# Value product and next scores between the halves of h, products of the high part first, one sum on VectorE

## The chip, the cores and the metric

The kernel runs on one core of a Trainium2 chip. The metric is the device time of one execution in microseconds (us), and runs of the kernel before are shown with their median. The engines are named as the trace names them: PE (TensorE's matmuls; PEld is its loading of weights), DVE (VectorE), ACT (ScalarE), POOL (GpSimd) and SP (SyncE, which here only issues transfers). All of them run in order, each its own list of instructions, and wait for one another by semaphores.

## The reference, cut to what matters

```
attention in chunks of 64:  scores = q k^T / 8; attn = softmax(scores); out = attn v
x  = out as (4608 tokens, 512)
h  = x @ w_in                                  # 512 -> 1024
sm = softmax(h);  u = h * sm
ln = (u - mean(u)) / sqrt(var(u) + 1e-6) * g
y  = ln @ w_out                                # 1024 -> 512
z  = y @ w_in2;  z = max(0.01 z, z);  out = z @ w_out2      # 512 -> 2048 -> 512
```

## The kernel before

The work has two parts. The first (attention, h, softmax, norm, y) goes over 36 tiles of 128 tokens, one tile at a time. The second (the last two products) goes over 6 groups of 768 tokens by a scheme of seven products in place of eight; the change doesn't touch it. Every float32 operand of a product is held as two rounded parts, high and low, and each product is made of three: high by high, high by low, low by high.

In the first part a round t of the loop holds work of several tiles at once, in an order that is written out by hand and that each engine keeps:

- `qk_mm(t+2)` (L349) makes scores, `softmax_a` and `softmax_b` (L362 to L373) the probabilities `es`: DVE takes maxima, differences and sums, ACT the exponentials, and POOL the last multiplication (L373, 128x512).
- `pt_mm` (L383) and `pt_copy` (L389, ACT) transpose the probabilities, `pv_mm` (L399) multiplies them by the values, `x_hi` (L413, ACT) and `x_lo` (L417, DVE) split the result x into its high and low part, `xs`. `attend(t)` is `pv_mm(t+1)` and the split, from t = 5 on also the scores, loads and `softmax_a` of tile t+3.
- `ff1_mm(t, half)` (L434) makes h: for t of 2 and more a half is 512 of the 1024 columns; for tiles 0 and 1 it is two of the four blocks of rows of w_in, for both column halves.
- `solu_max`, `solu_a`, `solu_b` (L449, L453, L457, L465) take the maximum of h's row, the exponentials (ACT) and their product with h (`us`, DVE), with sums over each column half in columns 8 to 11 of the small tile `z`. `solu_c` adds these sums of the halves on POOL (L479, two of them: the sum of the exponentials in column 1, that of the products in column 2) and gives the second to ACT, whose square (`sq`, L488) takes it as its bias. `solu_d` finishes the norm on POOL (L494 to L498).
- `lnT_mm` (L509) transposes the normed tile, `lnT_hi` (L520, ACT) and `lnT_lo` (L524, DVE) split it, `y1_group` (L536) makes 128 rows of y for 512 tokens, from t = 5 on one group a round, and ACT copies it out (`ys`, L544).
- In between, weights that arrive as float64 words are converted: ACT `magnitudes` (L101), DVE L108 to L118, POOL `by_g` (L171), ACT and POOL the split of w_out (L124, L125), DVE, ACT and POOL the blocks of the second part's weights (L189 to L195). Some rounds convert two pieces (`DOUBLE`).

Two sets of PSUM banks matter below: the outputs of `lnT_mm` and `y1_group` take turns in two banks called `ef`, and the transposed probabilities and x share one bank called `ptx`. Rounds 5, 9, 13, ... are called late: they copy and split the norm of tile t-2 before the rest, and make the first group of y of a block. The lines that are shown here and those of the profile are the same.

Of the kernel before, what the change touches and what calls it, by code (L numbers as in the profile page):

```python
# [14 lines left out]
ALU = mybir.AluOpType  # L15
# [8 lines left out]
T = NT // P  # L24
# [18 lines left out]
AHEAD = 5  # L43
# [9 lines left out]
def kernel(  # L53
# [252 lines left out]
    with tc.manual_schedule():  # L306

        with ExitStack() as phase:
# [107 lines left out]
                ps, x = x_ps.pop(t), xs[t]  # L416
                dve.tensor_tensor(x[:, 1], ps, x[:, 0].bitcast(F32), op=ALU.subtract)  # L417

            def ff1_mm(t, half):
                if t < 2:  # L420
                    ks, ns = ((0, 1), (2, 3))[half], (0, 1)
                else:
                    ks, ns = range(KD), (half,)
                for n in ns if t >= 2 or half == 0 else ():
                    if t == 1 and n == 1:
                        hs[t, n] = bank("ef", "h_ps")
                    else:
                        hs[t, n] = psh.tile([P, 512], F32, tag="h", name="h_ps")
                x = xs[t]
                for kk in ks:  # L430
                    w = slots["wi1", kk // 2].rearrange("p e (a n f) -> p e a n f", a=2, n=2)
                    for a, b in ((0, 0), (0, 1), (1, 0)):
                        for n in ns:
                            pe.matmul(  # L434
                                hs[t, n],
                                lhsT=x[:, a, kk, :],
                                rhs=w[:, b, kk % 2, n, :],
                                start=(kk == 0 and a == 0 and b == 0),
                                stop=(kk == KD - 1 and a == 1),
                            )  # L440
                if half == 1:
                    del xs[t]

            sol = {}
# [16 lines left out]
            def solu_b(t):  # L461
                z, u = sol[t], us[t]
                for n in range(2):
                    c = slice(n * 512, (n + 1) * 512)
                    dve.scalar_tensor_tensor(  # L465
                        u[:, c],
                        hs.pop((t, n)),
                        1.0 / FF1,
                        u[:, c],
                        op0=ALU.mult,  # L470
                        op1=ALU.mult,
                        accum_out=z[:, 10 + n : 11 + n],
                    )

            def solu_c(t):
                z, u = sol[t], us[t]
                for n in (1, 2):
                    a = 6 + 2 * n
                    pool.tensor_tensor(  # L479
                        z[:, n : n + 1], z[:, a : a + 1], z[:, a + 1 : a + 2], op=ALU.add  # L480
                    )
                pool.tensor_scalar(
                    z[:, 4:5], z[:, 1:2], 1e-9, (1e-6 * FF1 * LN_SCALE) ** 0.5, op0=ALU.add, op1=ALU.mult
                )
                pool.tensor_tensor(z[:, 5:6], z[:, 4:5], z[:, 4:5], op=ALU.mult)
                pool.tensor_scalar_mul(z[:, 0:1], z[:, 2:3], -1.0 / FF1)
                sq = wk.tile([P, FF1], BF16, tag="sq", bufs=1, name="sq")
                act.activation(  # L488
                    sq, u, AF.Square, scale=-float(FF1), bias=z[:, 2:3], accum_out=z[:, 3:4]
                )  # L490
# [63 lines left out]
            def attend(t):  # L554

                pv_mm(t + 1)
                if AHEAD <= t < T - 3:
                    qk_mm(t + 3)
                    load_qk(t + 4)
                x_split(t + 1)  # L560
                if AHEAD <= t < T - 3:
                    softmax_a(t + 3)
# [160 lines left out]
            for t in range(1, T + 2):  # L723
                if t == T:
                    att.close()
                    yp = ctx.enter_context(
                        tc.tile_pool(name="yp", bufs=1, side="right", reuse_waits="tile")
                    )
                    ws = ctx.enter_context(
                        tc.tile_pool(name="ws", bufs=WS, side="right", reuse_waits="tile")  # L730
                    )
                    for n in range(4):
                        y_load(0, n)
                    for _ in range(WS):
                        w_load()
                if t <= AHEAD:
                    load_qk(t + 3)
                load_v(t + 2)
                store_next()
                load_next(owed)  # L740
                owed = 0
                b, g = divmod(t - 5, 4)
                groups = [(b, g)] if 5 <= t < T else []
                if t == T - 1:
                    groups = []
                elif t == T:
                    groups = [(NB - 2, 2), (NB - 2, 3)]
                elif t == T + 1:
                    groups = [(NB - 1, m) for m in range(KD)]
                late = g == 0 or t == T - 1  # L750
                pieces = 0 if t in (1, 4) or t >= T - 2 else 2 if t in DOUBLE else 1
                if 0 < t <= AHEAD:
                    qk_mm(t + 2)
                if 1 <= t <= T:
                    if t < 3:
                        solu_max(t - 1, 0)
                    solu_max(t - 1, 1)
                    solu_a(t - 1)
                if t <= AHEAD:
                    softmax_a(t + 2)  # L760
                if t > AHEAD and not late:
                    take_magnitudes(pieces)
                if 1 < t < T:
                    ff1_mm(t, 0)
                if 1 <= t <= T:
                    solu_b(t - 1)
                if t + 1 < T:
                    pt_mm(t + 1)
                if t + 2 < T:
                    softmax_b(t + 2)  # L770
                if t <= AHEAD or (late and t < T - 1):
                    pt_copy(t + 1)
                if late and t >= 2:
                    lnT_mm(t - 2)
                    lnT_split(t - 2, 0)
                    lnT_split(t - 2, 1)
                if t > AHEAD:
                    if late:
                        take_magnitudes(pieces)
                    convert_a(pieces)  # L780
                    convert_b(pieces)
                if AHEAD < t < T - 1 and not late:
                    pt_copy(t + 1)
                if 1 < t < T:
                    solu_max(t, 0)
                if 1 <= t <= T:
                    solu_c(t - 1)
                    solu_d(t - 1)
                if t == T + 1:
                    y_split(0, 0)  # L790
                    for name in ("s1", "s3", "s2"):
                        y_sum(0, name)
                    y_split(0, 1)
                    y_sum(0, "s4")
                    for k in range(2, 7):
                        y_split(0, k)
                if groups and not late:
                    for bm in groups:
                        y1_group(*bm)
                    if t + 1 < T:  # L800
                        attend(t)
                    if t >= 2:
                        lnT_mm(t - 2)
                        lnT_split(t - 2, 0)
                        lnT_split(t - 2, 1)
                    if t < T:
                        ff1_mm(t, 1)
                    finish(pieces)
                else:
                    if t >= 2 and not late:  # L810
                        lnT_mm(t - 2)
                        for hf in range(2):
                            (lnT_hi if t < AHEAD else lnT_split)(t - 2, hf)
                    if AHEAD < t < T - 1:
                        attend(t)
                    if t < T:
                        ff1_mm(t, 1)
                    if t <= AHEAD:
                        attend(t)
                        if 2 <= t < AHEAD:  # L820
                            for hf in range(2):
                                lnT_lo(t - 2, hf)
                        finish()
                        take_magnitudes(pieces)
                        convert_a(pieces)
                        convert_b(pieces, load=t == AHEAD)
                        owed = pieces if t < AHEAD else 0
                    if t >= AHEAD:
                        finish(pieces)
                    for bm in groups:  # L830
                        y1_group(*bm)
# [295 lines left out]
```

## Time and profile before

| what | value |
|---|---|
| median of 3 runs | 1279.92 us (1279.71 to 1281.45) |
| the profiled execution's own time | 1279.53 us |
| span in its trace | 1277.7 us |
| PE busy | 1234.1 us, 97% of the span |
| DVE, ACT, POOL busy | 891.3, 572.9, 287.5 us |
| end of the first part on PE (first product of the second) | 568.6 us |

The span is the time from the first to the last instruction in the trace; the execution's own time is 1.8 us more. Busy time is summed over instructions of an engine. The second part runs on PE almost without a gap, so what can be seen of waiting lies in the first 569 us. A row of the timeline has the start, the length, the engine, the line and the operation, the tile it writes and those it reads; in brackets stands how long its engine sat idle before it and what ended that.

### The profile page before, as it was taken

How to read it: one execution, taken by the hardware profiler on the slowest of the kernel's cores; microseconds unless marked ns; L12 is line 12 of the kernel's file. 1: busy time of each engine (PE TensorE's matmuls, PEld its weight loads, DVE VectorE, ACT ScalarE, POOL GpSimd, SP SyncE). 2: the span in 40 equal slices, each digit the busy share in tenths (PEclk: the TensorE clock that was granted, in tenths of full speed). 3: DMA queues.
4: the chain of work that ended last, by engine and by line, in shares of the span. 5: the costliest groups of instructions: out<-in, count | busy, mean ns of one | idle time of the engine just before them, and what ended most of it. 6: DMA issues, size and time to landing. Idle time of an engine off the chain costs nothing.

```text
span 1277.7 us, 22962 instructions
## 1 busy us (share of the span) xinstructions
PE 1234.1 (97%) x8554; PEld 1094.5 (86%) x8554; DVE 891.3 (70%) x1567; ACT 572.9 (45%) x1078; POOL 287.5 (22%) x426
## 2 busy tenths in 40 slices
PE   5888999999999999999999999999999999999998
PEld 4666788878878887889989998998899899989987
DVE  8666678887887788445676677567757775775675
ACT  6553545554555555433434344235234433442351
POOL 0244455765664576400000000000000000000000
PEclk8998999999999999999999999999999999999999
DMA  7423355755676564529899988987898899789676
GB/s 246 149 69 116 116 179 169 259 175 172 203 240 199 157 189 151 206 80 325 267 307 295 303 243 257 316 287 241 277 316 257 264 294 304 241 260 300 205 214 198
DMA packets 171070, 288.83 MB, mean 226 GB/s; under 512 B 50000, under 2 KB 80720, under 8 KB 169936
## 3 DMA queue, kind: packets, MB, share of 16 engines
q1 hardware_dynamic: 170592, 286.78, 70.3%
q8 instruction: 69, 1.13, 0.3%
q10 hardware_dynamic: 368, 0.59, 0.1%
q14 instruction: 41, 0.34, 0.1%
HBM read 239.08 MB, written 48.23 MB: 225 GB/s over the span
## 4 chain that ended last, share of the span: by engine, by line
PE 80%; DVE 10%; ACT 4%; DMA 2%; issue 2%; POOL 2%; SPq 0%; POOLq 0%; ACTq 0%
PE h_ps L870 27%; PE o_ps L927 18%; PE y_ps L536 11%; PE o_ps L938 9%; PE h_ps L434 9%; PE x_ps L399 2%; DVE us L465 1%; PE ln_ps L509 1%; DMA kb<-in_k 1%; DVE lnT L524 1%; DVE wf L114 1%; DVE wf L108 1%; POOL es L373 1%; DVE wc L191 1%; DVE st L362 1%
## 5 line engine op out<-in xcount | busy, mean ns | idle before, releaser
L870 PE MATMUL h_ps<-yo,w_s 128*128 128x384 f32 x2016 | 351.0, 334 | 0.0
L870 PEld LDWEIGHTS h_ps<-yo,w_s 128*128 128x128 f32 x2016 | 349.3, 188 | 0.7
L927 PE MATMUL o_ps<-wo_s,yo 128*128 128x512 f32 (+1 forms) x1016 | 262.8, 393 | 0.0
L434 PE MATMUL h_ps<-wi,xs 128*128 128x512 f32 x864 | 214.8, 401 | 12.3 <-ACT xs L413 5.5
L536 PE MATMUL y_ps<-lnT,wo 128*128 128x512 f32 (+1 forms) x888 | 204.7, 387 | 1.1 <-POOL wo L125 0.8
L434 PEld LDWEIGHTS h_ps<-wi,xs 128*128 128x128 f32 x864 | 161.7, 192 | 49.3 <-DVE us L465 6.3
L927 PEld LDWEIGHTS o_ps<-wo_s,yo 128*128 128x128 f32 x1016 | 179.0, 188 | 28.7
L536 PEld LDWEIGHTS y_ps<-lnT,wo 128*128 128x128 f32 x888 | 161.6, 188 | 33.6 <-POOL wo L125 1.3
L938 PEld LDWEIGHTS o_ps<-wo_s,yo 128*128 128x128 f32 x1008 | 144.6, 188 | 15.6
L271 DVE TENSOR_TENSOR yo<-c,yo 128x768 fp32r<-128x768 f32 x144 | 132.5, 952 | 32.0 <-ACT yo L270 32.0
L938 PE MATMUL o_ps<-wo_s,yo 128*128 128x256 f32 x1008 | 149.7, 283 | 0.0
L849 ACT ACTIVATE c<-h_c 128x384 f32<-128x384 f32 x144 | 72.9, 526 | 127.7 <-DVE h_c L881 127.7
L881 DVE TENSOR_TENSOR h_u<-h_ps,h_p 128x384 f32<-128x384 f32 x96 | 53.3, 555 | 105.9 <-PE h_ps L870 99.2
L270 ACT ACTIVATE yo<-c 128x768 fp32r<-128x768 f32 x144 | 113.1, 838 | 7.1 <-DVE c L911 5.5
L488 ACT ACTIVATE sq<-us,z 128x1024 bf16<-128x1024 f32 x36 | 41.4, 1150 | 80.5 <-POOL z L479 80.5
L465 DVE SCALAR_TENSOR_TENSOR us<-h_ps,us 128x512 f32<-128x512 f32 x72 | 48.6, 690 | 35.0 <-ACT us L457 35.0
L373 POOL TENSOR_TENSOR es<-es,st 128x512 f32<-128x512 f32 x33 | 34.6, 1048 | 157.3 <-DVE st L372 148.0
L524 DVE TENSOR_TENSOR lnT<-ln_ps,lnT 128x512 fp32r<-128x512 f32 x72 | 45.8, 680 | 33.9 <-ACT lnT L520 33.9
L457 ACT ACTIVATE us<-h_ps,z 128x512 f32<-128x512 f32 x72 | 48.7, 682 | 39.1 <-DVE z L453 39.1
L270 ACT ACTIVATE yo<-a 128x768 fp32r<-128x768 f32 x36 | 30.0, 841 | 72.6 <-DVE a L265 72.6
L881 DVE TENSOR_TENSOR h_c<-h_ps,h_u 128x384 f32<-128x384 f32 x96 | 53.2, 554 | 13.1 <-PE h_ps L870 11.9
L417 DVE TENSOR_TENSOR xs<-x_ps,xs 128x512 fp32r<-128x512 f32 x36 | 24.7, 687 | 51.4 <-ACT xs L413 51.4
(89 smaller groups left out, 1415.9 us busy)
## 6 DMA issues: line engine op xcount, KB each, us to landing
w_s<-wi_d SPq DMA_DIRECT2D x336, 256.0 KB, 4.0
wo_s<-wo_d SPq DMA_DIRECT2D x168, 512.0 KB, 4.6
wi_d<-wi SPq DMA_DIRECT2D x8, 1792.0 KB, 6.4
wo_d<-wi SPq DMA_DIRECT2D x8, 1792.0 KB, 7.0
raw<-in_w_out SPq DMA_DIRECT2D x24, 512.0 KB, 5.1
raw<-in_w_in SPq DMA_DIRECT2D x23, 512.0 KB, 5.6
vbd<-in_v SPq DMA_DIRECT2D x72, 128.0 KB, 4.6
a<-y_d SPq DMA_DIRECT2D x24, 384.0 KB, 5.3
```

The lines of the kernel that those rows point to most:

```text
L270: act.activation(o[:, 0], x, AF.Copy)
L271: dve.tensor_tensor(o[:, 1], x, o[:, 0].bitcast(F32), op=ALU.subtract)
L434: pe.matmul(hs[t, n], lhsT=x[:, a, kk, :], rhs=w[:, b, kk % 2, n, :], start=(kk == 0 and a == 0 and b == 0), stop=(kk == KD - 1 and a == 1),)
L457: act.activation(u[:, c], hs[t, n], AF.Exp, bias=z[:, 0:1], accum_out=z[:, 8 + n : 9 + n])
L465: dve.scalar_tensor_tensor(u[:, c], hs.pop((t, n)), 1.0 / FF1, u[:, c], op0=ALU.mult, op1=ALU.mult, accum_out=z[:, 10 + n : 11 + n],)
L524: dve.tensor_tensor(dst[:, 1], ps, dst[:, 0].bitcast(F32), op=ALU.subtract)
L536: pe.matmul(ps[:, part], lhsT=w[:, a, kk % 4, m * P : (m + 1) * P], rhs=lnT[:, c, kk, pairs, :][:, part], start=(kk == 0 and a == 0 and c ...
L849: act.activation(blocks[block, j // 2][:, j % 2], src, AF.Prelu, alpha=0.01)
L870: pe.matmul(ps, lhsT=w[:, a, kk * P : (kk + 1) * P], rhs=y[:, c, kk, :], start=(first and kk == 0 and a == 0 and c == 0), stop=(kk == 1 an ...
L881: dve.tensor_tensor(o, ps, x, op=ALU.add)
L927: pe.matmul(ps[:, : 2 * P * (a.stop - a.start)], lhsT=x[:, 0, kk, m * P : (m + 1) * P], rhs=w[:, kk, a].rearrange("p a n -> p (a n)"), sta ...
L938: pe.matmul(sums[p % 2][m][:, : 2 * P], lhsT=x[:, 1, kk, m * P : (m + 1) * P], rhs=w[:, kk, 0], start=False, stop=(i == PAIRS - 1 and kk = ...
```

## The change

Three things are changed. `ff1_mm` runs through its blocks of rows twice, first for the two products of x's high part, then for that of its low part, where it took the three products of a block together. In rounds 2 to 5 `attend(t)` stands ahead of `ff1_mm(t, 1)` where it stood behind it, and in round 1 between the two blocks of that half; the later rounds had it ahead already. The sum of the halves' products (column 2 of `z`) is made on DVE, at the end of `solu_b`, where it was one of POOL's two additions in `solu_c`.

```diff
-            def ff1_mm(t, half):
+            def ff1_mm(t, half, ks=None):
                 if t < 2:
-                    ks, ns = ((0, 1), (2, 3))[half], (0, 1)
+                    ks, ns = ks or ((0, 1), (2, 3))[half], (0, 1)
...
-                for kk in ks:
-                    w = slots["wi1", kk // 2].rearrange("p e (a n f) -> p e a n f", a=2, n=2)
-                    for a, b in ((0, 0), (0, 1), (1, 0)):
-                        for n in ns:
-                            pe.matmul(
...
+                for terms in (((0, 0), (0, 1)), ((1, 0),)):
+                    for kk in ks:
+                        w = slots["wi1", kk // 2].rearrange("p e (a n f) -> p e a n f", a=2, n=2)
+                        for a, b in terms:
+                            for n in ns:
+                                pe.matmul(
...
+                dve.tensor_tensor(z[:, 2:3], z[:, 10:11], z[:, 11:12], op=ALU.add)
 
             def solu_c(t):
                 z, u = sol[t], us[t]
-                for n in (1, 2):
-                    a = 6 + 2 * n
-                    pool.tensor_tensor(
-                        z[:, n : n + 1], z[:, a : a + 1], z[:, a + 1 : a + 2], op=ALU.add
-                    )
+                pool.tensor_tensor(z[:, 1:2], z[:, 8:9], z[:, 9:10], op=ALU.add)
...
-                    if AHEAD < t < T - 1:
+                    if t == 1:
+                        ff1_mm(t, 1, (2,))
                         attend(t)
-                    if t < T:
+                        ff1_mm(t, 1, (3,))
+                    elif t < T - 1:
+                        attend(t)
+                    if 1 < t < T:
                         ff1_mm(t, 1)
                     if t <= AHEAD:
-                        attend(t)
```

On PE, in round 1 and the first half of round 2, before (s_ps are scores, pt_ps the transposed probabilities, h_ps the products of h, x_ps the value product, ln_ps the transposed norm):

```order
L383 MATMUL pt_ps<-ident,es 128x128 x4
L434 MATMUL h_ps<-wi_355,xs 128x512 x12
L399 MATMUL x_ps<-pt,vbd_104 64x64 x16
L349 MATMUL s_ps<-kb_102,qt 64x64 x16
L434 MATMUL h_ps<-wi_173,xs 128x512 x6
L434 MATMUL h_ps<-wi_355,xs 128x512 x6
L383 MATMUL pt_ps<-ident,es 128x128 x4
L509 MATMUL ln_ps<-ident,us 128x128 x8
L434 MATMUL h_ps<-wi_173,xs 128x512 x6
L434 MATMUL h_ps<-wi_355,xs 128x512 x6
L399 MATMUL x_ps<-pt,vbd_105 64x64 x16
L349 MATMUL s_ps<-kb_103,qt 64x64 x16
```

The same place of PE in the changed kernel:

```order
L383 MATMUL pt_ps<-ident,es 128x128 x4
L435 MATMUL h_ps<-wi_355,xs 128x512 x6
L399 MATMUL x_ps<-pt,vbd_104 64x64 x16
L435 MATMUL h_ps<-wi_355,xs 128x512 x6
L349 MATMUL s_ps<-kb_102,qt 64x64 x16
L435 MATMUL h_ps<-wi_173,xs 128x512 x4
L435 MATMUL h_ps<-wi_355,xs 128x512 x4
L435 MATMUL h_ps<-wi_173,xs 128x512 x2
L435 MATMUL h_ps<-wi_355,xs 128x512 x2
L383 MATMUL pt_ps<-ident,es 128x128 x4
L507 MATMUL ln_ps<-ident,us 128x128 x8
L399 MATMUL x_ps<-pt,vbd_105 64x64 x16
```

The value product of the next tile (x_ps) now stands between the halves of h in round 1, and in round 2 right behind the transposed norm, with the second half of h behind it; within a half the eight products of the high part stand ahead of the four of the low part.

On DVE in round 3, from the minimum of the negated maxima to the factors of the probabilities, before:

```order
L453 TENSOR_TENSOR z<-z 128x1
L362 TENSOR_REDUCE st_739<-s_ps 128x4 x2
L365 TENSOR_TENSOR es<-s_ps,st_739 128x4x64 x2
L465 SCALAR_TENSOR_TENSOR us,z<-h_ps,us 128x512 x2
L370 TENSOR_REDUCE st_739<-es 128x8
L371 TENSOR_SCALAR st_739<-st_739 128x8
L372 RECIPROCAL st_739<-st_739 128x8
```

The same place of DVE in the changed kernel:

```order
L454 TENSOR_TENSOR z<-z 128x1
L362 TENSOR_REDUCE st_739<-s_ps 128x4 x2
L365 TENSOR_TENSOR es<-s_ps,st_739 128x4x64 x2
L466 SCALAR_TENSOR_TENSOR us,z<-h_ps,us 128x512 x2
L475 TENSOR_TENSOR z<-z 128x1
L370 TENSOR_REDUCE st_739<-es 128x8
L371 TENSOR_SCALAR st_739<-st_739 128x8
L372 RECIPROCAL st_739<-st_739 128x8
```

One addition of 128x1 (L475) has come in behind the products `us`, ahead of the sum of the probabilities (L370); DVE has 36 of them, one for each tile, and POOL 36 fewer.

On POOL in the same round, the multiplication of the probabilities and what of the norm is queued behind it, before:

```order
L373 TENSOR_TENSOR es<-es,st_739 128x512
L479 TENSOR_TENSOR z<-z 128x1 x2
L482 TENSOR_SCALAR z<-z 128x1
L485 TENSOR_TENSOR z<-z 128x1
L486 TENSOR_SCALAR z<-z 128x1
L494 TENSOR_SCALAR z<-z 128x1
```

The same place of POOL in the changed kernel:

```order
L373 TENSOR_TENSOR es<-es,st_739 128x512
L479 TENSOR_TENSOR z<-z 128x1
L480 TENSOR_SCALAR z<-z 128x1
L483 TENSOR_TENSOR z<-z 128x1
L484 TENSOR_SCALAR z<-z 128x1
L492 TENSOR_SCALAR z<-z 128x1
```

Of the two additions behind the multiplication one is left, and it is not the one that ACT's square reads.

## Rows read from the trace of the kernel before

**Rows 1.** Windows by stage: busy us (x instructions) of PE, PEld, DVE, ACT, POOL; PEclk; DMA
```profile
37.00:102.00 65.00, 53.02 (x556) 40.95 (x554) 44.53 (x106) 31.94 (x70) 28.18 (x53) 1.00 0.32 96
102.00:141.00 39.00, 32.83 (x248) 26.69 (x249) 25.29 (x55) 17.67 (x38) 19.13 (x27) 0.87 0.42 131
141.00:569.00 428.00, 420.81 (x3487) 349.06 (x3486) 317.13 (x632) 218.27 (x428) 238.41 (x338) 1.00 0.56 178
```
**Rows 2.** Waits, 37 to 141 us: who for whom, us in total, times, longest
```profile
ACT sq L488 <- POOL z L479: 26.1, 7, 7.0
```
**Rows 3.** Chain that ended last, round 3: start us, us, what
```profile
63.23 0.61 DVE st L370
...
64.44 1.04 POOL es L373
...
65.82 1.24 ACT sq L488 x2
67.06 0.97 ACT lnT L520 x2
...
68.55 0.69 DVE xs L417
```
**Rows 4.** Timeline, 32 to 67 us
```profile
32.41 4.87 PE L434 MATMUL h_ps<-wi,xs 128*128 128x512 f32 x20 [1.18 <-DVE xs L417]
...
36.27 2.02 ACT L629 ACTIVATE es<-es,st 128x64 f32<-128x64 f32 x8 [0.54 <-DVE st L624]
...
55.41 0.69 DVE L417 TENSOR_TENSOR xs<-x_ps,xs 128x512 fp32r<-128x512 f32 x1 [3.73 <-ACT xs L413]
...
57.67 0.43 DVE L110 TENSOR_SCALAR wf<-wf 128x512 uint32<-128x512 uint32 x1
...
59.63 1.04 POOL L171 TENSOR_TENSOR wf<-wf,g_sb 128x512 f32<-128x512 f32 x1 [3.30 <-DVE wf L118]
...
60.19 0.50 DVE L453 TENSOR_TENSOR z<-z 128x1 f32<-128x1 f32 x1
...
62.59 0.59 ACT L389 ACTIVATE pt<-pt_ps 128x512 f32<-128x512 f32 x1
...
65.62 1.15 PE L399 MATMUL x_ps<-pt,vbd 128*64 128x64 f32 x32
```
**Rows 5.** Timeline, 84 to 143 us
```profile
102.02 5.30 PE L536 MATMUL y_ps<-lnT,wo 128*128 128x512 f32 x22 [0.83 <-POOL wo L125]
...
111.79 1.15 ACT L488 ACTIVATE sq<-us,z 128x1024 bf16<-128x1024 f32 x1 [6.97 <-POOL z L479]
...
113.57 1.11 PE L509 MATMUL ln_ps<-ident,us 128*128 128x128 f32 x4 [3.95 <-ACT ys L544]
...
132.66 1.11 PE L509 MATMUL ln_ps<-ident,us 128*128 128x128 f32 x4 [2.20 <-ACT ys L544]
...
142.29 1.15 DVE L110 TENSOR_SCALAR wf<-wf 128x512 uint32<-128x512 uint32 x1
```
**Rows 6.** Windows around PE's waits, columns as in the first group
```profile
59.00:63.00 4.00, 1.36 (x11) 1.09 (x10) 3.96 (x10) 2.27 (x6) 1.04 (x1) 1.00 0.50 157
...
112.20:119.00 6.80, 5.43 (x15) 4.47 (x16) 3.30 (x7) 4.44 (x9) 3.08 (x6) 0.50 0.73 228
...
132.70:136.10 3.40, 3.40 (x10) 2.85 (x11) 2.02 (x5) 1.32 (x3) 1.71 (x2) 0.50 0.80 258
```
**Rows 7.** Waits of PE, 141 to 569 us
```profile
PE ln_ps L509 <- ACT ys L544: 4.4, 3, 1.5
...
PE s_ps L349 <- DMA kb<-in_k: 0.9, 2, 0.7
```
**Rows 8.** Line L453, all of its instructions: ns min/median/max
```profile
L453 DVE TENSOR_TENSOR z<-z x36: 158/160/685, 38.4 to 534.8; 128x1 f32<-128x1 f32 x36
```
**Rows 9.** Timeline, 524 to 570 us: the second part's first loads and product
```profile
526.37 6.49 SPq L292 DMA_DIRECT2D w_s<-wi_d  x9
...
568.64 3.64 PE L870 MATMUL h_ps<-yo,w_s 128*128 128x384 f32 x20
```

More of the change, by code (lines that the diff above doesn't have):

```diff
@@ L429, in ff1_mm @@
                 x = xs[t]
-                for kk in ks:
-                    w = slots["wi1", kk // 2].rearrange("p e (a n f) -> p e a n f", a=2, n=2)
-                    for a, b in ((0, 0), (0, 1), (1, 0)):
-                        for n in ns:
-                            pe.matmul(
[L435 to L439, printed above, removed]
-                            )
-                if half == 1:
+                for terms in (((0, 0), (0, 1)), ((1, 0),)):
[4 more added lines that the diff above has]
+                                pe.matmul(
+                                    hs[t, n],
+                                    lhsT=x[:, a, kk, :],
+                                    rhs=w[:, b, kk % 2, n, :],
+                                    start=(kk == 0 and a == 0 and b == 0),
+                                    stop=(kk == KD - 1 and a == 1),
+                                )
+                if half == 1 and ks[-1] == KD - 1:
                     del xs[t]
@@ L473, in solu_b @@
                     )
+                dve.tensor_tensor(z[:, 2:3], z[:, 10:11], z[:, 11:12], op=ALU.add)
             def solu_c(t):
                 z, u = sol[t], us[t]
-                for n in (1, 2):
-                    a = 6 + 2 * n
-                    pool.tensor_tensor(
-                        z[:, n : n + 1], z[:, a : a + 1], z[:, a + 1 : a + 2], op=ALU.add
-                    )
+                pool.tensor_tensor(z[:, 1:2], z[:, 8:9], z[:, 9:10], op=ALU.add)
                 pool.tensor_scalar(
```

## The prediction

> **What bounds the kernel now.** I cut the span into stages first [rows 1]. From 569 us on, in the second part, PE is busy nearly all of the time and nothing is changed, so all gain or loss must come from the first part. There PE idles for 65.00 - 53.02 = 11.98 us in rounds 1 to 5 (37 to 102 us), for 39.00 - 32.83 = 6.17 us in rounds 6 and 7 (102 to 141 us), and for 428.00 - 420.81 = 7.19 us in all the later rounds. In the middle stage PE also runs at half clock (granted 0.50, which is 1.2 GHz) for 5.43 + 3.40 = 8.83 us of work, right behind its two long waits [rows 6]. At 2.4 GHz that work takes half, so the clock costs 4.41 us. The most that could be won is 11.98 + 6.17 + 4.41 + 7.19 = 29.8 us.
>
> Next, the waits of the first two stages: the largest of those that stand in front of something else is ACT's square, which waits for POOL's `z` 26.1 us in 7 rounds [rows 2]. The chain that ended last shows why this matters [rows 3]: in round 3 DVE ends `us` at 63.23, goes on to the sum of the probabilities, POOL multiplies them from 64.44, then does the additions of `z`, and the square starts at 65.82. What the square needs was there at 63.23; it waits 2.59 us for a POOL that is busy with something else. Behind it in ACT's order stand `lnT_hi` and `x_hi`, behind these DVE's `x_lo` (68.55), and behind that, on DVE, everything of the next round. From the `x_lo` of round 2 at 55.41 [rows 4] to that of round 3 is 13.14 us: 7.82 on DVE to 63.23, 2.59 on the way through POOL, 2.73 on ACT. This loop, not PE, sets the pace of rounds 1 to 5.
>
> In rounds 6 and 7 the same wait is longer, since a conversion that has DVE's end first is queued on POOL ahead of `z`: 6.97 us, square at 111.79 [rows 5]. Behind the square on ACT stands `ys`, which frees the bank for PE's transposes: hence PE's waits of 3.95 and 2.20 us, and the half clock behind each. In the later rounds three waits for `ys` are left, 4.4 us [rows 7].
>
> **The change part by part.** *The sum on DVE.* The changed program lets the square wait for DVE alone. In the loop above, the 2.59 us give way to the new addition. Its price comes from the row of the same form, the minimum of the maxima (L453, two columns of 128x1): 0.16 us in the median [rows 8], and 0.04 us for each of two handovers, 0.24 in all. So a round loses 2.35 us, 13.14 becomes 10.79.
>
> *The value product ahead of the second half of h.* Left where it was, it would end at 65.62 + 1.15 = 66.77 us in round 3 [rows 4], while `x_hi` could then start 2.2 us (square and `lnT_hi`) after the addition, at 63.47 + 2.21 = 65.68: about half of the gain would stay behind PE. Moved, it needs the copy `pt` (62.59 + 0.59 = 63.18) and ends by 64.6, hidden behind the square. The price is a new wait of PE, which has done the first half of h and the transposes by then and stands still for that copy. It costs nothing as long as DVE's loop is the longer one: of the 65.00 us of the stage 54.2 are left if 10.8 go (sum below), and PE has 53.02 us of work in it [rows 1]. So PE is near to being the next bound, its new waits are some 1 us over all rounds, more if busy time holds some waiting too, and none should be longer than the one that it replaces. That one goes: the second half of h waited for its bank, 4.00 - 1.36 = 2.64 us in round 3 [rows 6], and now follows when the bank is free. In round 5 the scores and loads of `attend` move with it, and the transfers behind them on SP go out earlier, against free buffers; cost nothing.
>
> *The products of the high part first.* At 32.41 PE waits 1.18 us for `x_lo` [rows 4]; four more products fit in there, 0.9 us. But ACT's probabilities run until 38.29 [rows 4], PE's next transposes and ACT's exponentials are queued behind these, so I count 0.2. Later `x_lo` ends before the low products are reached; nothing.
>
> *Sum of rounds 1 to 5.* Four rounds at 2.35 are 9.4; in round 5, where `lnT_hi` is ahead of the square and DVE's own work ends last, some 1.2 more; with the 0.2 it is 10.8. Against that, DVE's conversions in rounds 2 to 4 now fall on POOL's norm and weight splitting. L453 shows what that does: 0.50 us at 60.19, ending with POOL's L171 (59.63 + 1.04) [rows 4]; and L110 took 1.15 us at 142.29 [rows 5] where it took 0.43 at 57.67 [rows 4]. Two conversions that are held so, by 0.7 each, cost 1.4, and 2.8 if by twice that; I take 1.4, so **9.4 us** (bounds 8.0 and 10.8). The gate is round 6's first product of y with new weights, at 102.02 now [rows 5].
>
> GPSIMD Engine Reference, section Key points, in the Trainium skill says that GpSimd shares its SBUF interfaces with VectorE and contends with VectorE instructions that have two SBUF inputs; the new addition is one. The trace agrees (L453 at 0.50 beside POOL's L171, 0.16 alone). By that rule the addition would be dear wherever POOL is in an instruction as DVE ends `us`; at the worst row, 0.685 [rows 8], on all 36 it would be 36 x 0.52 = 19 us more of DVE, and the forecast 7 us or so later if the 13 rounds that hang on DVE (the first 7, and 3 pairs below) pay it.
>
> *Rounds 6 and 7.* The square can start when ACT is through its conversions and `pt`, some 7 us earlier; `ys` then follows PE's own product at once. Gone are 3.95 + 2.20 + 4.41 = 10.56 us, the clock because the waits ahead of its fall are gone. What is late next is the weights of the next group of y, which come by way of DVE, POOL, ACT and POOL again, and PE now asks for them earlier. The trace has that wait once, 0.83 us at 102.02 [rows 5], and in these two rounds not at all; between 0 and 1 us each I take 0.3, since the normed tile and both splits on POOL also come earlier with the square. **10.0 us** (bounds 8.5 and 10.6).
>
> *Later rounds.* The three waits for `ys`, 4.4 us, stand in rounds with two conversions, where DVE ends last, and so does the wait for keys, 0.9 us, whose load is queued on SP behind the store of `ys` [rows 7]. The addition comes twice into each such pair, and may be held there (0.16 to 0.685 each), which returns up to 0.9 a pair as a wait for `pt`, by the middle 0.5. Of 5.3 us **3.8** stay (bounds 2.6 and 5.3). In the rounds between, DVE is idle 428 - 317.13 = 110.9 us in 29 rounds, 3.8 a round, which hides 0.2. POOL has an addition less.
>
> *Sum.* 9.4 + 10.0 + 3.8 = 23.2 us, from the profiled execution's 1279.53 us: 1256.3. The median is 0.39 above that execution, so **1256.7 us**. With all bounds together 19.1 to 26.7 us: 1253 to 1261, and I give 1252.5 to 1261 for this case.
>
> **The rivals.** *DVE and POOL get in each other's way.* The loop has little slack left on either, and if conversions and additions are held more often than I count, rounds 1 to 5 give 5 us, the weights come later in rounds 6 and 7 (8 us), the pairs give 2: 15 us, 1265 (1261 to 1268). For it: L453 and L110 above. Against: POOL is busy only 28.18 of 65 us there [rows 1].
>
> *The square stays late.* If it is not released by the addition, for a wait that I don't see, only the reordering is left. In the loop, nothing of it comes ahead of the square, so 2 to 6 us by the bank of h and the start: about 1275. Against: it waits for DVE alone.
>
> *Given back at the second part.* If its first product waits for something that doesn't come earlier, the time stays at 1280. Against: the weights are asked for from 526.37 on, first used at 568.64 [rows 9], and the operands' splits follow the same engines.
>
> *Slower: the clock.* PE's new waits in rounds 1 to 4 could bring it to 1.2 GHz there. Each us of PE's work at half clock takes one more, so it takes 23.2 us of work to undo the gain; beyond that the kernel is slower, and with all of the 53.02 us of rounds 1 to 5 at that clock it would be 1280 + 53 - 23 = 1310. Against: the wait of 2.64 us in round 3 was followed by a clock of 1.00 [rows 6], and the slow stretches there last 6.8 and 3.4 us.
>
> **How the numbers follow.** The forecast has 0.70, the held VectorE 0.15, the late square 0.06, the second part 0.05, the clock 0.04. The range is that of the first two cases, 1252 to 1268; it leaves out the other three and a little of the first, 2 in 10. A measurement of this kernel tells a change of 0.2% (2.6 us) from none. Faster by more: 0.70 + 0.15 + 0.06 = 0.91; within it 0.05; slower 0.04.
>
> **What would show it.** The square should start 0.3 us after `us` in rounds 1 to 4, and never name POOL as what ended its wait; `x_lo` should come every 10.8 us; the two waits of PE for `ys` in rounds 6 and 7, and the half clock behind them, should be gone, and so the three later ones; the second part should start at about 545 us. The new addition should take 0.16 us in the median. If PE's wait for `pt` in rounds 1 to 5 is over 3 us each, or the granted clock falls there, or the addition is near 0.7 us, the prediction is wrong at that step.

## The result, and the profile after

The changed kernel takes 1264.13 us in the median of 4 runs (1262.47 to 1266.24) against 1280.68 (1279.71 to 1282.34) beside it: a ratio of 0.987, with a 95% interval of 0.985 to 0.989. That is 16.6 us less; the forecast was 23.2 less, 1256.7 us, in a range of 1252 to 1268. The profiled execution took 1262.47 us, its span is 1260.7. Line numbers behind 434 are shifted by up to two.

The windows of the three stages, whose ends lie 12, 16 and 17 us earlier than in [rows 1] (columns as there):

```profile
37.00:90.00 53.00, 46.74 (x510) 37.63 (x503) 45.38 (x108) 30.18 (x66) 24.15 (x45) 1.00 0.35 105
90.00:125.00 35.00, 35.00 (x281) 28.97 (x280) 27.75 (x61) 20.43 (x42) 22.37 (x28) 1.00 0.55 166
125.00:552.00 427.00, 418.86 (x3475) 348.21 (x3474) 319.01 (x660) 217.94 (x427) 236.92 (x309) 1.00 0.56 178
```

PE stands still for 6.26 us in the first stage, where it stood 11.98, not at all in the second, at full clock, and for 8.14 us in the third, more than the 7.19 of before. The waits that answer to [rows 2], 37 to 126 us (in total, times, longest):

```profile
PE x_ps L399 <- ACT pt L389: 5.8, 3, 3.5
...
ACT sq L486 <- DVE z L475: 0.6, 2, 0.3
```

The square's 26.1 us for POOL have become 0.6 for DVE. What PE waits for is now the copy `pt`. The timeline of rounds 2 to 4 shows why, beside [rows 4]:

```profile
50.87 0.69 DVE L417 TENSOR_TENSOR xs<-x_ps,xs 128x512 fp32r<-128x512 f32 x1 [1.71 <-ACT xs L413]
...
59.01 1.15 PE L399 MATMUL x_ps<-pt,vbd 128*64 128x64 f32 x32 [1.67 <-ACT pt L389]
59.26 1.15 ACT L486 ACTIVATE sq<-us,z 128x1024 bf16<-128x1024 f32 x1 [0.30 <-DVE z L475]
...
61.99 0.69 DVE L417 TENSOR_TENSOR xs<-x_ps,xs 128x512 fp32r<-128x512 f32 x1 [1.22 <-ACT xs L413]
63.49 1.21 POOL L496 TENSOR_SCALAR us<-us,z 128x1024 f32<-128x1024 f32 x1
63.79 1.18 DVE L108 TENSOR_SCALAR wf<-wf 128x512 f32<-128x512 f32 x1
64.66 1.46 POOL L125 TENSOR_TENSOR wo<-wf,wo 128x512 fp32r<-128x512 f32 x1
65.01 1.40 DVE L110 TENSOR_SCALAR wf<-wf 128x512 uint32<-128x512 uint32 x1
...
71.53 1.15 PE L399 MATMUL x_ps<-pt,vbd 128*64 128x64 f32 x32 [3.54 <-ACT pt L389]
74.56 0.69 DVE L417 TENSOR_TENSOR xs<-x_ps,xs 128x512 fp32r<-128x512 f32 x1 [1.22 <-ACT xs L413]
```

The reader is to see two rounds: `x_lo` (L417) of round 3 comes 11.12 us after that of round 2, where the forecast's loop gives 10.79, and that of round 4 another 12.57 us later, because the first two instructions of round 3's conversion (L108, L110) sit behind one of POOL's each, 1.18 and 1.40 us in place of 0.42 and 0.43. PE's wait of 3.54 us in round 4 is the end of that.

The addition, all of its instructions (minimum, median, longest in ns), against L453 in [rows 8]:

```profile
L475 DVE TENSOR_TENSOR z<-z x36: 158/160/428, 40.5 to 520.6; 128x1 f32<-128x1 f32 x36
```

In the later rounds, 126 to 560 us, PE waits for one thing alone; before it waited for `ys` and keys too [rows 7]:

```profile
PE x_ps L399 <- ACT pt L389: 8.1, 9, 2.1
```

Three of these nine are 2.10 us long, in rounds 17, 25 and 33, the others 0.3. The timeline around the first:

```profile
241.49 1.15 PE L399 MATMUL x_ps<-pt,vbd 128*64 128x64 f32 x32 [0.29 <-ACT pt L389]
...
244.81 0.69 DVE L118 SCALAR_TENSOR_TENSOR wf<-raw,wf 128x512 uint32<-128x512 uint32 x1
...
249.59 0.60 PE L383 MATMUL pt_ps<-ident,es 128*128 128x128 f32 x4
...
251.13 0.16 DVE L454 TENSOR_TENSOR z<-z 128x1 f32<-128x1 f32 x1
251.32 0.69 ACT L458 ACTIVATE us<-h_ps,z 128x512 f32<-128x512 f32 x1 [1.66 <-DVE z L454]
...
252.66 0.59 ACT L389 ACTIVATE pt<-pt_ps 128x512 f32<-128x512 f32 x1
...
253.31 1.25 PE L399 MATMUL x_ps<-pt,vbd 128*64 128x64 f32 x32 [2.10 <-ACT pt L389]
...
254.49 1.13 PE L349 MATMUL s_ps<-kb,qt 64*64 64x64 f32 x32
```

The transposes were done at 250.2; ACT's copy of them stands behind two exponentials, which wait for DVE's minimum (L454), and DVE is late from a conversion (its last instruction is at 244.81). The scores behind the wait took 1.13 us where they take 0.69: PE was at 1.2 GHz (a granted clock of 0.50 from 254.3 to 257.5 us). The second part begins here, against 568.64 in [rows 9]:

```profile
551.54 1.73 PE L871 MATMUL h_ps<-yo,w_s 128*128 128x384 f32 x9
```

To divide the gain of 17.10 us up to there I compare the start of the value product of each round in the two traces. Rounds 1 to 5 (up to the product of tile 7, 107.25 against 99.25) gave 8.00, rounds 6 and 7 (tile 9, 146.22 against 127.52) 10.70, and the rounds behind took 1.60 back. The forecast had 9.4, 10.0 and 3.8. The experiments use the same three figures, called stages A, B and C, from their traces against the trace of the kernel before. That is one execution of each, so a stretch at half clock in one of them, some 1.6 us, shows in a stage whatever the edit.

### The profile page after: what moved, and what is told of

Read it like the earlier page. It is cut to its first block, busy times and chain, and to the rows that moved or that the text cites. A ratio compares the mean times of both kernels' runs of the same rounds, so it can differ in the third digit from the quotient of the medians.

```text
span 1260.7 us, 22964 instructions
## 1 busy us (share of the span) xinstructions
PE 1228.4 (97%) x8554; PEld 1092.5 (87%) x8554; DVE 897.1 (71%) x1603; ACT 573.3 (45%) x1078; POOL 285.2 (23%) x390
## 3 DMA queue, kind: packets, MB, share of 16 engines
q8 instruction: 69, 1.13, 0.4%
## 4 chain that ended last, share of the span: by engine, by line
PE 85%; DVE 8%; ACT 4%; DMA 1%; issue 1%; SPq 0%; ACTq 0%
PE h_ps L871 28%; PE o_ps L928 19%; PE y_ps L534 13%; PE h_ps L435 10%; PE o_ps L939 10%; PE x_ps L399 2%; PE ln_ps L507 2%; PE s_ps L349 1%; DVE lnT L522 1%; ACT us L458 1%; PE pt_ps L383 1%; DVE us L466 1%; DVE wf L114 1%; DVE wf L118 1%; DVE wf L108 1%
## 5 line engine op out<-in xcount | busy, mean ns | idle before, releaser
L435 PE MATMUL h_ps<-wi,xs 128*128 128x512 f32 x864 | 211.2, 397 | 1.0 <-ACT xs L413 0.7
L366 ACT ACTIVATE es<-es 128x512 f32<-128x512 f32 x33 | 20.8, 632 | 89.4 <-DVE es L365 89.4
L399 PEld LDWEIGHTS x_ps<-pt,vbd 128*64 128x64 f32 x1152 | 37.4, 140 | 26.7 <-ACT pt L389 18.4
```

What stands on the lines that cost most here:

```text
L399: pe.matmul(ps[e * D : (e + 1) * D, i, c * D : (c + 1) * D], lhsT=vv[:, i, c, e], rhs=pp[:, i, c * D : (c + 1) * D], start=True, stop=True,)
L435: pe.matmul(hs[t, n], lhsT=x[:, a, kk, :], rhs=w[:, b, kk % 2, n, :], start=(kk == 0 and a == 0 and b == 0), stop=(kk == KD - 1 and a == 1),)
```

## The experiments

Each edit is shown against the changed kernel; times are medians, with the ratio to the kernel before on the same chip and its interval.

**The parts of the change, alone.** The first has only the new sum, the second only the new place of `attend`, the third only the new order of products, the fourth the first two. The core of the first, where order of products and place of `attend` go back:

```diff
-                for terms in (((0, 0), (0, 1)), ((1, 0),)):
...
-                    elif t < T - 1:
-                        attend(t)
+                    if t < T:
+                        ff1_mm(t, 1)
+                    if t <= AHEAD:
+                        attend(t)
```

> The kernel before with the sum on VectorE alone; the order of the value product and of the products stays. Theory (the square's release carries the gain): the square starts 0.3 us after us, x_hi then waits for the value product, which stands behind the second half of h, so a round of 1 to 5 loses some 1.25 us in place of 2.35; rounds 6 and 7 give their 10.6 us whole, the later rounds return 1.6. In all 13 to 15 us, 1266 us. Rival (the gain is the new order on TensorE): under 4 us, 1277 or more.

Measured: 1269.87 us, 0.9935 [0.9915, 0.9955]; stages A 1.44, B 10.32, C -2.16. PE in round 3:

```profile
60.50 4.61 PE L434 MATMUL h_ps<-wi,xs 128*128 128x512 f32 x12 [2.62 <-DVE us L465]
65.04 1.15 PE L399 MATMUL x_ps<-pt,vbd 128*64 128x64 f32 x32
```

The square starts 0.25 us after the addition does, but the value product stays behind the second half of h, which waits for its bank. From one `x_lo` to the next it is 13.65 us here, not less than the 13.14 of before. Of these, some 1.6 us are the clock: the twelve products take 4.61 us where they take 3.02 at full speed. Without that the loop would be some 12.05 us, 1.1 less than before (an estimate from these rows). Rounds 6 and 7 give nearly all of their gain to the sum alone. The second kernel, where the sum goes back to POOL and the products to their old order:

```diff
-                dve.tensor_tensor(z[:, 2:3], z[:, 10:11], z[:, 11:12], op=ALU.add)
...
+                for n in (1, 2):
+                    a = 6 + 2 * n
+                    pool.tensor_tensor(
```

> The kernel before with the value product moved ahead of the second half of h in rounds 1 to 5, sum and products as before. Theory: x_hi is held by the square and the square by GpSimd, so nothing comes earlier: within 1 us of before, 1280 us, x_lo still every 13.1 us. Rival: 8 us or more in rounds 1 to 5, 1272 us.

Measured: 1276.82 us, 0.999 [0.998, 1.0001]; A 0.09, B 2.80, C 0.08. Each `x_lo` of rounds 1 to 4 comes within 0.1 us of its time before. The 2.80 are not the move's: the clock is 0.96 in rounds 6 and 7, in place of 0.87, since PE is at half clock for one stretch of 3.4 us in this execution, where the traced one of the kernel before has 6.8 and 3.4. The third, where sum and place go back:

```diff
-                dve.tensor_tensor(z[:, 2:3], z[:, 10:11], z[:, 11:12], op=ALU.add)
...
-                    if t == 1:
-                        ff1_mm(t, 1, (2,))
```

> The kernel before with the products of the high part first, nothing else. Theory: the wait of 1.18 us near 32 us shrinks to 0.3, but ScalarE's probabilities hide most of it: 0.2 to 0.6 us, 1280 us. Rival: the 0.9 us are kept whole and more in each round where x_lo was waited for, 2 to 3 us.

Measured: 1277.02 us, 0.9987 [0.9975, 1.0]; A 0.17, B 2.82 (the same shorter stretches), C -0.43. The `x_lo` of round 1 comes 13.03 us after the one before it, in place of 13.80: 0.77 us, and waits with half clock behind them take it back in rounds 3 and 4. The fourth, where only the order of products goes back:

```diff
-                for terms in (((0, 0), (0, 1)), ((1, 0),)):
-                    for kk in ks:
+                for kk in ks:
```

> The changed kernel with the products in the old order. Theory: all but 0.6 us of the gain, within 1 us of the changed kernel. Rival: as for the products alone, 2 to 3 us slower than the changed kernel.

Measured: 1265.82 us, 0.9898 [0.988, 0.9917]; A 4.96, B 10.73, C -2.03. The median is 1.7 us above the changed kernel's, but the intervals of the two ratios overlap; in the traces the stage that differs is A. There PE waits 1.19 us for the first `x_lo`, as before, and its twenty products take 6.38 us, where they took 4.87 in [rows 4], at a clock of 0.74 in that window (32.0 to 38.5 us); a second such stretch follows its wait of 3.51 us in round 4. So in stage A the sum needs the move and the move needs the sum, and the order of products is worth 0.8 us and a wait that the clock may fall behind. In stage B the sum does it alone.

**Where the addition is.** ACT makes the sum, ahead of its square.

```diff
-                dve.tensor_tensor(z[:, 2:3], z[:, 10:11], z[:, 11:12], op=ALU.add)
...
+                act.activation(z[:, 2:3], z[:, 10:11], AF.Identity, bias=z[:, 11:12])
```

> The changed kernel with the sum of the halves' products on ACT, ahead of its square, and none of it on DVE or POOL. Theory one (in the double conversions of the later rounds VectorE is the bound and the addition lengthens its chain, by up to 0.5 us where GpSimd holds it): PE's wait for the transposed probabilities in rounds 17, 25 and 33 falls from 2.1 to about 1.0 us each, 1260 to 1262 us. Theory two (those waits come from PE asking earlier, not from the addition): they stay at 2.1 us, 1264 us, and an activation more ahead of every square costs nothing.

Measured: 1259.93 us, 0.9857 [0.9842, 0.9871]; A 6.81, B 10.71, C +2.30. PE's waits in the later rounds:

```profile
PE x_ps L399 <- ACT pt L389: 5.1, 3, 1.7
PE s_ps L349 <- DMA kb<-in_k: 1.4, 2, 1.1
```

The three waits of 2.10 are 1.71, the six of 0.3 us are gone, and in this execution no half clock came behind them. Theory one, though with less off each long wait than it said: 0.39 us by the addition, 1.71 without it. A is 1.2 less than the changed kernel's, by one half-clock stretch behind round 4's wait. The addition made twice:

```diff
+                dve.tensor_tensor(z[:, 12:13], z[:, 10:11], z[:, 11:12], op=ALU.add)
```

> The changed kernel with the addition on VectorE made twice, the second into a column that nobody reads. Theory one (VectorE's chain is the bound in rounds 1 to 4 and in the three pairs): 0.1 us more in each of rounds 1 to 4 and 0.2 to 0.4 us in each of four rounds by three, 1266 to 1268 us. Theory two (the addition is hidden): no change, 1264 us.

Measured: 1264.9 us, 0.9893 [0.9878, 0.9908], not to be told from the changed kernel. Each round that hangs on DVE is 0.07 to 0.08 us longer, 0.8 us in all with the half clock left out. Theory one fell in its size: of the 36 second additions none took longer than 0.155 us. What the first one pays beyond its 0.16 us is the hold by POOL.

**The double conversions.** Where do the waits of 2.10 us come from?

```diff
-DOUBLE = (5, 6, 7, 14, 15, 22, 23, 30, 31)
+DOUBLE = (5, 6, 7, 11, 15, 19, 23, 27, 31)
```

> The changed kernel with the double conversions in rounds 11, 15, 19, 23, 27 and 31 in place of 14, 15, 22, 23, 30 and 31, so that no two stand side by side after round 7. Theory one (two in a row are what VectorE can't take in): the three pairs of waits, 0.29 and 2.1 us, and the half clock behind them go, and no others come: 1257 to 1259 us. Rival (a single double conversion is already too much for a round): each of the six leaves a wait of about 1 us, and the time stays within 2 us of 1264.

Measured: 1277.28 us, 0.9982 [0.9973, 0.999], 13 us slower than the changed kernel; C -15.25.

```profile
PE x_ps L399 <- ACT pt L389: 15.9, 9, 3.0
```

Both expectations failed. The round with a single double conversion, 15, is followed by the same waits as the pair 14 and 15 (0.35 in round 16, 2.10 in round 17), and round 11 by 2.74 us in round 13. Every wait of 2 us or more stands in a late round, two behind a double conversion, and half clock follows five of the six. So it is not two in a row that hurt, and more places make more waits. A third choice of rounds:

```diff
-DOUBLE = (5, 6, 7, 14, 15, 22, 23, 30, 31)
+DOUBLE = (5, 6, 7, 10, 14, 18, 22, 26, 30)
```

> The changed kernel with the later double conversions in rounds 10, 14, 18, 22, 26 and 30, each three rounds ahead of a late round. The run with them in 11, 15, ... showed the wait of 2.1 to 3.0 us in every late round that comes two rounds behind a double conversion, and the one with 14 and 15 has it no worse than with 15 alone. Theory (a round more for VectorE to catch up before the late round, which asks early for the transposed probabilities): the waits of 2.1 us shrink to 0.3 us, six of them, and no half clock follows: about 1257 us. Rival (VectorE is short in any round near a double conversion): six waits of about 1 us, 1262 us or more.

Measured: 1264.1 us, 0.9877 [0.9864, 0.9891]; C -2.07. Six waits again, 2.05 and 1.02 us by turns, 9.2 us in all: a round more is not enough to catch up, and the late round pays what is left. The theory's time failed by 7 us, and "two rounds behind a double conversion" was not the rule: here all six waits come three rounds behind one. The same edit on the kernel before:

> The kernel before with the later double conversions in rounds 10, 14, 18, 22, 26 and 30. Theory (its three waits for ys of 1.5 us are VectorE's lag behind the same double conversions, which the changed kernel only meets elsewhere): they go, and the wait for keys with them, 4 to 5 us, 1275 us. Rival (they are GpSimd's lateness with the square, as the forecast had it): they stay wherever a double conversion stands, six of them, 1280 to 1285 us.

Measured: 1283.56 us, 1.0031 [1.0019, 1.0043], slower. The three waits for `ys` of 1.5 us fell to 0.55, but waits of 1.98 us for `pt` came in rounds 13, 21 and 29. The theory's time is refuted; that the waits for `ys` depend on where DVE's double conversions stand is shown, and so is that the kernel before pays in its late rounds too.

**ACT's order in the late rounds.** The copy stands ahead of the exponentials of h.

```diff
+                    if early:
+                        pt_copy(t + 1)
+                        solu_a(t - 1)
                     solu_b(t - 1)
...
-                if t <= AHEAD or (late and t < T - 1):
+                if t <= AHEAD:
                     pt_copy(t + 1)
```

> The changed kernel with ACT's copy of the transposed probabilities ahead of its two exponentials of h in the late rounds from 9 on, where it stood behind them; the order of PE and DVE stays. The trace of the changed kernel has these exponentials wait for VectorE's minimum at 251.13, and the copy, whose own operand is there at 250.2, run only at 252.66; so PE's 2.10 us go by way of ACT's order. Theory: the three waits of 2.1 us and the three of 0.33 go and PE's next products of h find their bank free, or wait at most 0.5 us for it: 6 to 7 us less, and no half clock behind, 1256 to 1258 us. Rival (VectorE's lag itself bounds these rounds, by whichever wait): PE waits as long a little later, for h's bank or the transposed norm, and the time is 1262 to 1264 us.

Measured: 1262.42 us, 0.9879 [0.9862, 0.9895]; C -0.04. In round 17:

```profile
246.36 0.69 DVE L118 SCALAR_TENSOR_TENSOR wf<-raw,wf 128x512 uint32<-128x512 uint32 x1
247.12 0.56 SPq L93 DMA_DIRECT2D raw<-in_w_in  x1
...
248.89 0.46 SPq L328 DMA_DIRECT2D kb<-in_k  x1
...
251.87 0.60 ACT L389 ACTIVATE pt<-pt_ps 128x512 f32<-128x512 f32 x1 [0.66 <-PE pt_ps L383]
255.21 0.69 PE L349 MATMUL s_ps<-kb,qt 64*64 64x64 f32 x32 [1.36 <-DMA kb<-in_k]
```

The copy is early and the waits of 2.1 us for it are gone; PE meets the load of keys (0.68 to 2.21 us, 4.2 in all) a little later. That load is queued on SP behind one that goes out 0.07 us after DVE's conversion ends, and so is late with DVE. ACT's order was the way of the wait; the lag of DVE is its cause, as the rival said, by a wait that I had not named. The median is no other than the changed kernel's.

**The held conversion.** Up to round 5, POOL's split of the piece before stands behind DVE's conversion of the new one.

```diff
-                        finish()
+                        n = len(done)
                         take_magnitudes(pieces)
                         convert_a(pieces)
                         convert_b(pieces, load=t == AHEAD)
+                        finish(n)
```

> The changed kernel with the split of the piece converted a round before set behind the conversion of the new piece in rounds up to 5, so that GpSimd's subtraction of 1.3 to 1.5 us doesn't run beside VectorE's conversion. Theory (the hold of the conversion in round 3 lengthens the round): the second instruction of the conversion takes 0.43 us in place of 1.40, PE's wait of 3.5 us in round 3 falls to about 2.6, and the time to about 1263. Rival (the first weights of y are then late): PE waits at its first product of y, in round 5 or 6, and the time is 1264 or more.

Measured: 1262.65 us, 0.9876 [0.9862, 0.9891]; A 9.18, B 10.70.

```profile
63.27 1.20 POOL L496 TENSOR_SCALAR us<-us,z 128x1024 f32<-128x1024 f32 x1
63.58 1.18 DVE L108 TENSOR_SCALAR wf<-wf 128x512 f32<-128x512 f32 x1
64.80 0.43 DVE L110 TENSOR_SCALAR wf<-wf 128x512 uint32<-128x512 uint32 x1
...
67.76 1.27 POOL L125 TENSOR_TENSOR wo<-wf,wo 128x512 fp32r<-128x512 f32 x1
70.36 1.15 PE L399 MATMUL x_ps<-pt,vbd 128*64 128x64 f32 x32 [2.57 <-ACT pt L389]
```

L110 is back at 0.43, PE's wait at 2.57, and the stage 1.18 us shorter, as expected (the wait that the expectation puts in round 3, where the conversion is, stands in round 4); the first instruction still sits behind L496. The medians, 1.5 us apart with overlapping intervals, don't show it. B is as before the edit, so the weights are not late.

**All together**: the sum on ACT, the later split, and the double conversions as in the run with 10, 14, 18.

```diff
-DOUBLE = (5, 6, 7, 14, 15, 22, 23, 30, 31)
+DOUBLE = (5, 6, 7, 10, 14, 18, 22, 26, 30)
...
-                dve.tensor_tensor(z[:, 2:3], z[:, 10:11], z[:, 11:12], op=ALU.add)
...
+                        finish(n)
```

> The last together with the sum on ACT and the later split of w_out's pieces. If the three are independent: 1.2 us less in round 3 and up to 0.3 us in each late round than the kernel with the double conversions moved alone, 1255 to 1256 us. Rival (what one leaves another has already taken): the same time as that kernel.

Measured: 1260.04 us, 0.9843 [0.9829, 0.9856]. 4 us less than with the conversions alone, where 3.0 were expected (1.2 in round 3 and six times 0.3), but no less than the sum on ACT alone, 1259.93: the later split and the conversions' new places together add nothing to it that the medians show, and 1255 to 1256 us was wrong. The three waits of 2.04 us in rounds 13, 21 and 29 stay; of those of 1.02 us one of 0.15 is left.

## Why the prediction was right or wrong

**The square and the loop**: right. The square starts 0.2 to 0.3 us after `us` in rounds 1, 3 and 4 and 0.8 in round 2, behind the copy `pt`; POOL ends none of its waits, and the new addition took the 0.16 us of L453 in the median.

**Rounds 1 to 5**, 9.4 forecast, 8.0 measured, at the lower bound, and that in an execution without half clock there: three runs whose program is the same up to there (the double conversions in other rounds, twice, and the copy first) gave 6.50, 6.65 and 6.61, below the bound, with a stretch of it in each. Round 3's loop took 11.12 for 10.79 us, and round 5 gave the 1.2 that was counted. The 2.35 us were taken from round 3 for all four rounds; the rounds differ (2.93, 1.73, 2.02 and 0.80 us from `x_lo` to `x_lo`). The last of these is the held conversion: 1.73 us in one round, against 1.4 in the sum, and the run with the later split shows 1.0 to 1.2 of it to be L125's. Behind it my mark of 3 us for PE's wait was passed, 3.54, so the step "none should be longer than the one that it replaces" was wrong; PE's new waits are 5.8 us over these rounds, where I had some 1.

The Trainium skill, SBUF — State Buffer, section Who interferes with whom, says that a VectorE `tensor_scalar` can run in a two-port mode, that GpSimd and such an instruction lock each other out, the one that issues first keeping the ports for all of its time, and that a VectorE instruction with two SBUF inputs contends with a GpSimd instruction that reads SBUF. The trace agrees, as far as ends tell: L496 ends at 64.70 and L108, begun at 63.79, ends 0.27 us later, and L110 ends 0.29 us after L125. At L475 too: 0.40 us at 224.69, ending at 225.09, with POOL's L195 through at 225.07. Of the 36 additions 13 are held, to between 0.31 and 0.43 us, each until 0.01 to 0.02 us behind the end of an L195 that began before it; the 23 others took 0.16, and POOL was in none of its long instructions then. So the rule of the Trainium skill that the prediction cites is borne out beside POOL's long instructions; beside one of 128x1 the addition took 0.16 three times. The 19 us did not come because POOL was in a long instruction in 13 rounds alone, and a hold added 0.15 to 0.27 us, not 0.52.

**The move**: right that it is needed. With the sum alone the loop of rounds 2 to 4 was hardly shorter, or longer (9.87, 13.65 and 13.65 us, against 9.95, 13.14 and 13.37), but in rounds 3 and 4 half clock took some 1.6 us of each; the 1.1 us that would be left without it in round 3 agree with "about half of the gain would stay behind PE". That the clock would take them back was not in the forecast.

**Products of the high part first**: 0.2 forecast, 0.77 in the run with it alone. I looked at what PE's next transposes wait for, but the loop runs over DVE: the maximum of h came 0.9 us earlier (36.30 against 37.18 in the run with the sum alone), and with it `x_lo`.

**Rounds 6 and 7**, 10.0 forecast, 10.70 measured: both waits for `ys` and the half clock are gone, and of the 0.3 us each for weights nothing came. Some 2.8 us of this stage hang on the execution of the kernel before that was traced: the runs with the move alone and the products alone were that much shorter here, without any part in it, for less time at half clock.

**Later rounds**, 3.8 forecast, -1.6 measured: the step that failed, 5.4 of the 6.1 us that are missing. "Of 5.3 us 3.8 stay" took the waits for `ys` as time that the square's lateness cost. They are gone, as are those for keys, but those for `pt` grew from 1.9 us (six) to 8.1 (nine); in the kernel before DVE was catching up while PE waited. There the value product of round 17 waits 0.31 us, behind 1.48 for `ys` in round 16; now it is 2.10, behind 0.29. The `x_lo` of rounds 12 and 17, and these waits, in the kernel before:

```profile
205.48 0.69 DVE L417 TENSOR_TENSOR xs<-x_ps,xs 128x512 fp32r<-128x512 f32 x1 [0.41 <-ACT xs L413]
...
263.94 0.66 PE L509 MATMUL ln_ps<-ident,us 128*128 128x128 f32 x4 [1.48 <-ACT ys L544]
...
271.71 1.15 PE L399 MATMUL x_ps<-pt,vbd 128*64 128x64 f32 x32 [0.31 <-ACT pt L389]
...
276.92 0.67 DVE L417 TENSOR_TENSOR xs<-x_ps,xs 128x512 fp32r<-128x512 f32 x1
```

The same `x_lo` in the changed kernel:

```profile
186.77 0.68 DVE L417 TENSOR_TENSOR xs<-x_ps,xs 128x512 fp32r<-128x512 f32 x1
...
258.70 0.67 DVE L417 TENSOR_TENSOR xs<-x_ps,xs 128x512 fp32r<-128x512 f32 x1
```

These five rounds take 71.44 us before and 71.93 now, and around the second pair 71.41 and 71.93: the same but for 0.5 us, though PE waits elsewhere. It is 71.93 with the sum alone too, 72.09 with the copy first, 72.16 with the addition made twice and 70.93 with the sum on ACT. So a chain through DVE sets their pace, and taking one wait of PE away there brought another. Its busy time would not have told: DVE is idle for 2.2 to 2.9 us in each of these rounds before, in part behind ACT, through which the chain runs as well.

From round 15's value product to round 18's the second and third pair take 0.2 and 0.4 us longer than before, the first 1.8, of which 1.5 is the half clock. Three runs say the same of the waits: putting the double conversions elsewhere moves them, taking the addition off DVE shortens them, and opening ACT's way to the copy makes PE wait for a load that goes out behind DVE's conversion. Of the term in the sum, the addition's part was small by half: 0.5 a pair was taken and up to 0.9 allowed, and the sum on ACT takes 1.0 off these five rounds. What stays open is the size, why a double conversion ahead of round 13 leaves 2.05 and one ahead of round 17 1.02.

**The clock** was put aside as a rival that could make the kernel slower, and was no term. It costs 1.5 us in the later rounds of the profiled execution; in rounds 1 to 5 of that one it stayed at 1.00, but seven of the nine kernels here that have sum and move show a stretch behind round 4's wait.

## What to carry to other kernels

A wait of the busiest engine can be the time in which another catches up. Before counting it as gain, take the time from one mark of the other engine (here `x_lo`) to the same mark some rounds later, in rounds with such waits, and ask what the busiest engine would meet if it came there earlier. Idle time of the other engine does not settle it: here it had 2.2 to 2.9 us a round, and the gain was nothing. And a loop that is timed in one round should be timed in each: the rounds of this prologue gave from 0.80 to 2.93 us.

A small instruction is priced by what holds it: a second addition cost 0.08 us of VectorE's chain, as nothing held it, and the first took some 0.40 where GpSimd was in a long instruction.

## What the runs showed of the hardware

How long PE waits didn't decide whether its clock fell. In the 14 traces there are 56 waits of PE of 2 us or more from 30 us on, ahead of the second part. In the 4 us from the end of each, the mean granted clock was 0.50 to 0.69 behind 30 and 1.00 behind 26. The changed kernel's own wait of 3.54 us was followed by 1.00 and a wait of 2.10 us by 0.61:

```profile
71.50:75.50 4.00, 3.96 (x44) 3.19 (x44) 2.68 (x9) 3.22 (x6) 2.20 (x7) 1.00 0.48 149
253.30:257.30 4.00, 3.99 (x68) 3.47 (x69) 3.83 (x11) 3.10 (x6) 2.21 (x4) 0.62 0.02 6
371.00:375.00 4.00, 3.95 (x73) 3.37 (x74) 3.83 (x11) 3.15 (x6) 2.17 (x4) 1.00 0.13 21
```

(windows of 4 us, columns as in [rows 1]). One such stretch costs 1.5 to 1.6 us, read from five runs behind round 4's wait (from `x_lo` to `x_lo` 9.89 to 10.00 us with it, 8.40 and 8.41 in the two without). The same program meets them or not: of the three equal waits of 2.10 us in the changed kernel one was followed by it, and its wait of 3.54 us was not, where the three runs that are the same program up to there, with 3.50 to 3.52, all fell. Nor does it take so long a wait: behind 1.18 us at 32 us the kernel before stayed at 1.00, and behind 1.19 the run with the old order of products was at 0.74.

Runs of the changed kernel lie 3.8 us apart, but their mean granted clock is 0.996 in all four. A stretch of 3.4 us at half clock would take 0.0014 off that (an estimate: 1.7 of 1262 us), so stretches don't make the spread. What does is open.
